# An attention-and-SwiGLU kernel on one Trainium2 core: the opening's order written out by hand, and one weight sum moved from tile zero to tile one

## The chip, the cores and the metric

One Trainium2 chip, one of its cores. The metric is the device time of one execution in microseconds. The kernel before takes 905.18 us, the median of three runs (903.3, 905.18 and 905.21).

The core has five engines with instruction streams of their own: TensorE (PE: matmuls and transposes), VectorE (DVE), ScalarE (ACT), GpSimd (POOL) and SyncE (SP), which here only issues DMA transfers. They wait for each other through semaphores.

## The reference

Chunked softmax attention, its heads joined to rows of 512 features, an RMS norm, and a SwiGLU layer:

```python
B, H, S, D = 8, 8, 576, 64; chunk = 64
# attention: each chunk of 64 tokens of a head looks at itself alone
scores = scale * np.matmul(q_c, k_c.transpose(0, 1, 2, 4, 3))   # 64 x 64 each
scores = scores - np.max(scores, axis=-1, keepdims=True)
attn = np.exp(scores)
attn = attn / (np.sum(attn, axis=-1, keepdims=True) + 1e-09)
out = np.matmul(attn, v_c)
x = out.reshape(B, H, S, D).transpose(0, 2, 1, 3).reshape(4608, 512)
# SwiGLU
rms = np.sqrt(np.mean(x * x, axis=-1, keepdims=True) + 1e-06)
xn = x / rms * rms_g
g = xn @ w_gate                       # 512 -> 1536
silu = g * (1.0 / (1.0 + np.exp(-g)))
val = xn @ w_val                      # 512 -> 1536
return silu * val @ w_out             # 1536 -> 512
```

All data are float32.

## The kernel before

**Tiles.** The 4608 tokens are cut into nine tiles of 512. Attention works in *units* of 256 tokens, two *subtiles* of 128 each: tile zero has units 0 and 1 (subtiles 0 to 3), tile one units 2 and 3, tile two units 4 and 5, and so on. The 1536 hidden features are twelve blocks f of 128.

**Precision.** Tokens and weights are split into a high and a low part (`xh`, `xl`; `parts` of a weight holds both), and a product takes three matmuls: high x high, high x low, low x high. One block `up(f)` is 24 matmuls, 12 for the gate (`ps_g`) and 12 for the value (`ps_v`). Then ScalarE takes the Silu of `ps_g` into `sg`, VectorE multiplies it with `ps_v`, ScalarE casts the high part `gh`, VectorE subtracts for the low part `gl`, and TensorE does `down(f)`, 12 matmuls into `acc`.

**Weights.** The weights arrive in 18 *pairs* in the order up f, up f+1, out f/2: one load of 1 MB each into a `raw` buffer (`conv_load`, issued AHEAD = 4 pairs ahead on SP's queue). Their conversion into parts takes these steps: ScalarE makes the absolute value (L189) and scales the low words (L190) in `conv_start`; VectorE clamps (L198), shifts (L199), joins the words (L200, L203) and ScalarE casts the high part (L214) in `conv_join`; VectorE subtracts for the low part (L220, the *remainder*) in `conv_end`. `conv_step` does the load for pair n+4, the start of pair n+1, the join of n and the end of n−1. Block up(f) needs the remainder of its pair. Buffers: 3 for `w`, 18 for `parts`, so that all converted weights stay on the chip.

**The opening.** q and k of unit 0 come in four pieces of 256 KB, q on SP's queue and k on ScalarE's (L254, L255). Subtiles 0 to 3 go through scores, softmax (a maximum and a subtraction on VectorE, one Exp on ScalarE, a sum on VectorE), transposes of the result, values, a scale by the sum (`norm`, L482), a sum of squares on ScalarE (L470), the mean on VectorE (L471), a power on GpSimd (L473), a scale on ScalarE (L488), transposes of the tokens (`x_transpose_unit`, L554) and their split (`x_split`: xh on ScalarE L523, xl on VectorE L524). The scores of subtiles 2 and 3 share one pair of PSUM banks (`s2`), two transposes of a unit share one buffer `eT`. No order is written down here: a list scheduler chooses each engine's order from the program below and from its own costs. `conv_step(EARLY)` with EARLY = 3 stands behind it.

```python
    s0, s1, s2 = (two_banks(p, "ps_s") for p in (ps_a, ps_h, ps_acc))
    scores(0, s0)
    scores(1, s1)
    softmax(0)
    softmax(1)
    ...
    x_transpose_unit(1)
    conv_start(0)
    conv_step(EARLY)
```

**Tile zero** is a plain loop over f: `gated(f)` (up, gate), pieces of the attention of unit 2 and unit 3, `save_out` and `save_up` (stores of converted weights for later tiles), the sums of output weights, `down(f-1)`. Within the loop the same list scheduler sets the order. Unit 2's four stages (scores with `softmax_rows`, transposes, values with `norm_unit`, scale) stand at f = 0, 2, 3, 4, unit 3's at 5, 7, 8, 9. `softmax_rows` has 32 Exp of 128x64 elements on ScalarE (L309), each with its sum; ScalarE loads another function table when it goes from Silu to Exp and back. `out_sides(i)` combines output weights of pair i for a later product: a sum (L659), four totals (L667), a cast (L671) and a remainder (L672). EARLY_SUMS = 2 of them stand in tile zero, at f = 9 and 10.

**Tiles one and two** run under `tc.manual_schedule`: within it each engine's order is that of the program text. They consist of 48 steps (`half`, called after each half block), and tables say at which step a piece of other work stands: UNIT_AT (eleven pieces for each of the units 4 to 9), SIDE_AT (sums of weights on GpSimd, `sides`), SUM_AT (the rest of `out_sides`). Behind them come three pairs of tiles whose matmuls are seven products in place of eight.

## Time and profile before

| | us | share of the span |
|---|---|---|
| median of three runs | 905.18 | |
| profiled execution | 903.54 | |
| its span | 901.8 | |
| PE busy | 875.2 | 97% |
| DVE busy | 672.1 | 75% |
| ACT busy | 438.1 | 49% |
| POOL busy | 171.6 | 19% |

The span reaches from the first to the last instruction that the profile shows in one profiled execution; that execution's own time is 1.7 us longer. Busy times are sums over the whole span, over stages with different limits, so the same engine can be idle in one stage and full in another. In the rows of the profile, a line begins with the start in microseconds (or with a stretch a:b), then the duration, engine, source line, operation and, in the form out<-in, the tiles; in square brackets stands how long the engine was idle just before, and what ended that. Rows of a stretch have the busy time of PE, PEld (weight loads), DVE, ACT and POOL, then the granted clock of TensorE, the busy share of the DMA engines and GB/s. Rows of groups end in the count.

### The profile page before, as it was taken

How to read it: one execution, taken by the hardware profiler on the slowest of the kernel's cores; microseconds unless marked ns; L12 is line 12 of the kernel's file. 1: busy time of each engine (PE TensorE's matmuls, PEld its weight loads, DVE VectorE, ACT ScalarE, POOL GpSimd, SP SyncE). 2: the span in 40 equal slices, each digit the busy share in tenths (PEclk: the TensorE clock that was granted, in tenths of full speed). 3: DMA queues.
4: the chain of work that ended last, by engine and by line, in shares of the span. 5: the costliest groups of instructions: out<-in, count | busy, mean ns of one | idle time of the engine just before them, and what ended most of it. 6: DMA issues, size and time to landing. Idle time of an engine off the chain costs nothing.

```text
span 901.8 us, 17138 instructions
## 1 busy us (share of the span) xinstructions
PE 875.2 (97%) x6792; PEld 715.4 (79%) x6792; DVE 672.1 (75%) x1083; ACT 438.1 (49%) x733; POOL 171.6 (19%) x213
## 2 busy tenths in 40 slices
PE   5799999999999999999999999999999999999998
PEld 4588878877888888888877888888878888888886
DVE  6999996788686887876577988756679974345885
ACT  5997944446353663433355644334536532112452
POOL 0100005395670000112221001122210002111000
PEclk9999999999999999999999999999999999999999
DMA  9698966879879967489877884898689677445623
GB/s 358 267 376 311 312 242 218 268 240 289 252 232 312 293 240 266 162 308 350 259 271 233 302 300 164 303 291 316 238 255 330 256 297 266 152 156 191 217 72 116
DMA packets 96512, 231.82 MB, mean 257 GB/s; under 512 B 7344, under 2 KB 63664, under 8 KB 81072
## 3 DMA queue, kind: packets, MB, share of 16 engines
q1 hardware_dynamic: 95376, 230.19, 73.9%
q8 instruction: 54, 0.88, 0.4%
q10 hardware_dynamic: 1056, 0.52, 0.2%
q14 instruction: 26, 0.21, 0.1%
HBM read 171.97 MB, written 58.72 MB: 256 GB/s over the span
## 4 chain that ended last, share of the span: by engine, by line
PE 74%; DVE 8%; issue 6%; ACT 6%; DMA 4%; POOL 1%; SPq 1%; ACTq 0%; DVEq 0%; POOLq 0%
PE ps_a L794 10%; PE ps_c L794 10%; PE ps_b L794 10%; PE ps_a L975 7%; PE ps_b L975 7%; PE ps_c L975 6%; PE ps_d L794 5%; PE ps_g L606 5%; PE ps_v L606 4%; PE ps_d L975 4%; PE ps_s L269 1%; PE ps_o L392 1%; DMA wr<-wsd 1%; PE acc L629 1%; DVE ab L723 1%
## 5 line engine op out<-in xcount | busy, mean ns | idle before, releaser
L894 ACT CAST gh<-g 128x512 fp32r<-128x512 f32 x140 | 81.7, 620 | 75.5 <-PE ps_b L975 21.3
L895 DVE TENSOR_TENSOR gl<-g,gh 128x512 fp32r<-128x512 f32 x140 | 95.3, 688 | 30.3 <-ACT gh L894 29.3
L794 PE MATMUL ps_c<-xp,wr 128*128 128x512 f32 x432 | 104.7, 391 | 0.0
L794 PE MATMUL ps_b<-xp,wr 128*128 128x512 f32 x432 | 104.4, 391 | 0.0
L794 PE MATMUL ps_a<-xp,wr 128*128 128x512 f32 x432 | 103.7, 390 | 0.4 <-DMA wr<-wsd 0.4
L794 PEld LDWEIGHTS ps_a<-xp,wr 128*128 128x128 f32 x432 | 80.9, 188 | 17.6 <-issue 0.8
L794 PEld LDWEIGHTS ps_c<-xp,wr 128*128 128x128 f32 x432 | 80.7, 188 | 17.1
L794 PEld LDWEIGHTS ps_b<-xp,wr 128*128 128x128 f32 x432 | 80.6, 188 | 16.9
L859 POOL TENSOR_TENSOR g<-c,c 128x512 f32<-128x512 f32 x18 | 23.2, 1291 | 359.1 <-DVE c L855 269.0
L606 PE MATMUL ps_g<-xh,parts 128*128 128x512 f32 x192 | 65.8, 396 | 1.1 <-ACT sg L619 1.1
L606 PE MATMUL ps_v<-xh,parts 128*128 128x512 f32 x192 | 66.2, 398 | 0.0
L975 PE MATMUL ps_a<-gh,wo 128*128 128x512 f32 x176 | 55.9, 389 | 0.0
L794 PE MATMUL ps_d<-xp,wr 128*128 128x512 f32 x216 | 51.9, 389 | 0.0
L975 PE MATMUL ps_c<-gh,wo 128*128 128x512 f32 x160 | 51.1, 392 | 0.2 <-ACT gh L894 0.2
L975 PE MATMUL ps_b<-gh,wo 128*128 128x512 f32 x160 | 50.5, 389 | 0.0
L794 PEld LDWEIGHTS ps_d<-xp,wr 128*128 128x128 f32 x216 | 40.5, 188 | 8.4
L937 DVE TENSOR_TENSOR g<-g 128x512 f32<-128x512 f32 x68 | 46.6, 686 | 0.0
L835 ACT ACTIVATE c<-c 128x512 f32<-128x512 f32 x18 | 11.4, 635 | 68.1 <-DVE c L855 68.0
L606 PEld LDWEIGHTS ps_v<-xh,parts 128*128 128x128 f32 x192 | 36.3, 189 | 10.1 <-issue 2.1
L606 PEld LDWEIGHTS ps_g<-xh,parts 128*128 128x128 f32 x192 | 36.5, 190 | 9.6 <-ACT sg L619 1.6
L844 DVE TENSOR_TENSOR u<-ps_b,p 128x512 f32<-128x512 f32 x36 | 24.0, 685 | 25.2 <-PE ps_b L794 24.0
L695 POOL TENSOR_TENSOR ab<-parts 128x256 f32<-128x256 f32 x48 | 37.3, 810 | 23.5 <-DVE xl L524 23.5
(176 smaller groups left out, 1872.3 us busy)
## 6 DMA issues: line engine op xcount, KB each, us to landing
wr<-wsd SPq DMA_DIRECT2D x63, 1024.0 KB, 8.5
qk<-qk_dram SPq DMA_DIRECT2D x17, 1024.0 KB, 6.9
wo<-wol SPq DMA_DIRECT2D x16, 1024.0 KB, 8.0
raw<-w_up_dram SPq DMA_DIRECT2D x12, 1024.0 KB, 13.0
wo<-wod SPq DMA_DIRECT2D x12, 1024.0 KB, 9.4
vt<-v_dram SPq DMA_DIRECT2D x18, 512.0 KB, 5.8
wsd<-parts SPq DMA_DIRECT2D x18, 512.0 KB, 8.3
wo<-wol SPq DMA_DIRECT2D x16, 512.0 KB, 7.6
```

Source lines behind the costliest of these rows:

```text
L269: nc.tensor.matmul(st["s"][j][c * CH : (c + 1) * CH, pr], st["q"][rows, pr, tok : tok + CH], st["k"][rows, pr, tok : tok + CH], start=True ...
L392: nc.tensor.matmul(st["o"][(2 * c + t) * Q : (2 * c + t + 1) * Q, h * D : (h + 1) * D], eT[rows, c, t, h], vt[rows, c, h], start=True, sto ...
L606: nc.tensor.matmul(ps[k], a, b[dt], start=(dt == 0 and i == 0), stop=(dt == NDT - 1 and i == 2), skip_group_check=True,)
L695: return nc.gpsimd.tensor_tensor(out, one, two, op=op)
L794: nc.tensor.matmul(ps, w[:, a, m, cols], xp[:, b, kt], start=start and kt == 0 and i == 0, stop=stop and kt == 1 and i == 2, skip_group_ch ...
L835: nc.scalar.activation(t, t if src is None else src, AF.Silu)
L844: nc.vector.tensor_tensor(kp["u2"], b["b"], kp["p1"], op=add)
L859: nc.gpsimd.tensor_tensor(g[1][1], kp["c22"], kept[0]["c22"], op=mult)
L894: nc.scalar.copy(gh, src)
L895: nc.vector.tensor_tensor(gl, src, gh.bitcast(F32), op=ALU.subtract)
L937: nc.vector.tensor_tensor(out, one, two, op=ALU.subtract)
L975: nc.tensor.matmul(ps[m][INTO[p]], w[:, m, a], parts[c], start=p in FROM and i == 0 and j == 0, stop=p in LAST and i == NPR - 1 and j == 2 ...
```

## The change

1. The opening is wrapped in a manual schedule of all five engines, and its text is written in a new order. Softmax is cut into `softmax_less`, `softmax_exp`, `softmax_sum` and `softmax_turned` (the reciprocal, once for both subtiles of a unit); `norm` into `norm`, `norm_square` and `norm_scale`; the conversion into `conv_abs`, `conv_low`, `conv_clamp`, `conv_words`, `conv_high`. The mean of squares is taken on GpSimd in front of the power.
2. q and k are laid out so that each subtile is one load of 512 KB (`load_sub`), four in all, all on SP's queue. The scores have four pairs of banks, and the transposes of the opening (`later=True`) go to buffers of `gh` and `gl`.
3. Only pair 0 is converted in the opening, and pair 1 is started. For pairs 2 to 7, ScalarE's first steps are ordered behind the last split of tokens (`tokens_first`).
4. `up_first` takes the place of `up` for f = 0: high x high of gate and value first, then low weights, then low tokens.
5. In tile zero, the stages of unit 2 stand at f = 1, 3, 4, 5 and of unit 3 at 6, 8, 9, 10 (UNITS_AT).
6. EARLY_SUMS goes from 2 to 1: `out_sides(0)` stands at f = 10, and `out_sides(1)` at step 2 of tile one.
7. Two rows of UNIT_AT (units 6 and 7) are changed, from their third number on by five to seven steps.

```diff
+UNITS_AT = {1: (2, 0), 3: (2, 1), 4: (2, 2), 5: (2, 3), 6: (3, 0), 8: (3, 1), 9: (3, 2), 10: (3, 3)}
 UNIT_AT = (
...
-    (5, 10, 16, 12, 14, 16, 25, 27, 27, 28, 31),
-    (11, 15, 27, 17, 19, 27, 32, 34, 34, 35, 38),
+    (5, 10, 13, 12, 14, 15, 18, 20, 20, 21, 25),
+    (11, 15, 20, 17, 19, 21, 26, 28, 28, 29, 32),
...
-SUM_AT = 0, 0, 7, 12, 26, 32
+SUM_AT = 0, 2, 7, 12, 26, 32
-EARLY_SUMS = 2
+EARLY_SUMS = 1
...
+    def tokens_first(ins, n):
+        if 1 < n <= LATER:
+            info = mybir.DependencyInfo(mybir.DependencyClass.NoSync, mybir.DependencyReason.DATA)
+            tc.add_manual_dep(ins.ins, first_last[0].ins.name, info, reason="tokens are split first")
...
+    def load_sub(i, t):
+        t = t.rearrange("p (w a t) -> p w a t", w=2, t=P)
+        nc.sync.dma_start(t, qk[i // 2][:, i % 2])
+        state[i] = {"q": t[:, 0], "k": t[:, 1]}
...
+    def up_first():
+        pg, pv = bank(ps_h, "ps_g"), bank(ps_h, "ps_v")
+        for i in range(3):
+            for ps, wh, wl in ((pg, wgh, wgl), (pv, wvh, wvl)):
+                a, b = ((wh, xh), (wl, xh), (wh, xl))[i]
+                for dt in range(NDT):
+                    nc.tensor.matmul(ps, a[0][:, dt * P : (dt + 1) * P], b[dt], ...)
+        return pg, pv
...
+    first_ordered = tc.manual_schedule(engines={*engines, mybir.EngineType.Pool})
+    first_ordered.__enter__()
+    for i in range(2):
+        load_sub(i, x[:, 2 * i : 2 * i + 2].rearrange("p s c -> p (s c)"))
+    t = io.tile([P, 2, 2, NPAIR, P], F32, tag="qk", bufs=1, name="qk")
+    for s in range(2):
+        load_sub(2 + s, t[:, s].rearrange("p w a t -> p (w a t)"))
+    load_values(0)
     conv_load(0)
+    nc.sync.dma_start(g_col, rms_g)
     load_values(1)
+    for n in range(1, AHEAD + 1):
         conv_load(n)
+    s0, s1, s2, s3 = (two_banks(p, "ps_s") for p in (ps_a, ps_h, ps_acc, ps_acc))
     scores(0, s0)
     scores(1, s1)
+    for i in range(2):
+        softmax_less(i)
+        softmax_exp(i)
+    copied = att_transpose(0, later=True)
+    scores(2, s2)
+    softmax_sum(0)
+    copied()
+    copied = att_transpose(1, later=True)
+    scores(3, s3)
+    softmax_sum(1)
+    softmax_turned(0)
+    copied()
+    softmax_less(2)
+    softmax_exp(2)
+    conv_abs(0)
...
+    att_values(3, o)
+    norm_scale(0)
+    norm(2)
+    norm_square(2)
+    norm_scale(1)
+    for half in range(2):
+        x_transpose_half(0, half, ps_a)
+    norm(3)
+    norm_square(3)
+    conv_words(0)
+    x_split_half(0, 0)
+    norm_scale(2)
+    x_split_half(0, 1)
+    conv_high(0)
+    norm_scale(3)
+    for half in range(2):
+        x_transpose_half(1, half, ps_acc)
+    conv_end(0)
+    for half in range(2):
+        x_split_half(1, half)
+    conv_start(1)
+    first_ordered.__exit__(None, None, None)
+    conv_step(EARLY - 1)
...
     for f in range(NF):
         g = gated(f, CONVS[f % 2], conv_step)
-        if f in (0, 5):
-            u = 2 + (f == 5)
+        u, stage = UNITS_AT.get(f, (None, None))
+        if stage == 0:
```

In the rows below the operation of an engine stands with its line, its output and inputs, the shape, and how often it stands in a row; line numbers of the two kernels differ. TensorE, from the last transposes of the opening into up(0), before; `xh_119` to `xh_122` are the high parts of the four blocks of 128 features, `xl_123` to `xl_126` the low ones:

```order
L554 MATMUL ps_x<-ident,x 128x128 x8
L565 MATMUL ps_g<-xh_119,parts 128x512
L565 MATMUL ps_v<-xh_119,parts 128x512
L565 MATMUL ps_g<-xl_123,parts 128x512
L565 MATMUL ps_g<-xh_119,parts 128x512
L565 MATMUL ps_v<-xl_123,parts 128x512
L565 MATMUL ps_v<-xh_119,parts 128x512
L565 MATMUL ps_g<-xh_120,parts 128x512
L565 MATMUL ps_v<-xh_120,parts 128x512
L565 MATMUL ps_g<-xl_124,parts 128x512
```

and after:

```order
L597 MATMUL ps_x<-ident,x 128x128 x16
L627 MATMUL ps_g<-xh_119,parts 128x512
L627 MATMUL ps_v<-xh_119,parts 128x512
L627 MATMUL ps_g<-xh_120,parts 128x512
L627 MATMUL ps_v<-xh_120,parts 128x512
L627 MATMUL ps_g<-xh_121,parts 128x512
L627 MATMUL ps_v<-xh_121,parts 128x512
L296 MATMUL ps_s_564<-qk 64x64 x2
L296 MATMUL ps_s_565<-qk 64x64
L627 MATMUL ps_g<-xh_122,parts 128x512
L627 MATMUL ps_v<-xh_122,parts 128x512
L627 MATMUL ps_g<-xh_119,parts 128x512
```

Before, up(0) takes the three products of one feature block after another; now it takes the high products of all four blocks first and the low parts of the tokens last, and the scores of unit 2 begin within it. The last eight transposes of the tokens stood alone ahead of it, and now all sixteen stand there together.

ScalarE, tile zero, around the 32 Exp of unit 2 (`e`, by rows of scores in two banks), before:

```order
L583 ACTIVATE sg<-ps_g 128x512
L309 ACT_TABLE_LOAD
L309 ACTIVATE e,rs_u<-ps_s_509,mx_u 128x64 x4
L309 ACTIVATE e,rs_u<-ps_s_510,mx_u 128x64 x3
L588 CAST gh<-sg 128x512
L309 ACTIVATE e,rs_u<-ps_s_510,mx_u 128x64
L309 ACTIVATE e,rs_u<-ps_s_509,mx_u 128x64 x4
L309 ACTIVATE e,rs_u<-ps_s_510,mx_u 128x64 x4
L214 CAST parts<-w 128x1024
L189 ACTIVATE w<-raw 128x1024
L583 ACT_TABLE_LOAD
L583 ACTIVATE sg<-ps_g 128x512
```

and after:

```order
L344 ACT_TABLE_LOAD
L344 ACTIVATE e,rs_u<-ps_s_564,mx_u 128x64
L649 ACT_TABLE_LOAD
L649 ACTIVATE sg<-ps_g 128x512
L344 ACT_TABLE_LOAD
L344 ACTIVATE e,rs_u<-ps_s_564,mx_u 128x64
L654 CAST gh<-sg 128x512
L344 ACTIVATE e,rs_u<-ps_s_564,mx_u 128x64 x2
L344 ACTIVATE e,rs_u<-ps_s_565,mx_u 128x64 x4
L344 ACTIVATE e,rs_u<-ps_s_564,mx_u 128x64 x4
L344 ACTIVATE e,rs_u<-ps_s_565,mx_u 128x64 x4
L237 CAST parts<-w 128x1024
```

A Silu (`sg`) now stands within the block of Exp, behind its first one, with a table load on each side of it; before, the Silu stood ahead of the block. The Exp block also stands later in the row of casts of `parts` and weight steps (`w`).

SyncE, its queue of loads and stores from weight pair 3 on (counted from 0) (`raw` is a weight load, `qk` and `vt` q, k and v of a unit, `wsd` and `wod` stores of converted weights), before:

```order
L181 DMA raw<-w_up_dram 128x1024 x2
L181 DMA raw<-w_out_dram 128x1024
L239 DMA qk<-qk_dram 128x2048
L181 DMA raw<-w_up_dram 128x1024 x2
L245 DMA vt<-v_dram 128x1024
L688 DMA wod<-parts 128x2048
L181 DMA raw<-w_out_dram 128x1024
L239 DMA qk<-qk_dram 128x2048
L245 DMA vt<-v_dram 128x1024
L685 DMA wsd<-parts 128x4x256
```

and after:

```order
L183 DMA raw<-w_up_dram 128x1024 x2
L269 DMA qk<-qk_dram 128x2048
L183 DMA raw<-w_out_dram 128x1024
L275 DMA vt<-v_dram 128x1024 x2
L751 DMA wsd<-parts 128x4x256
L183 DMA raw<-w_up_dram 128x1024
L269 DMA qk<-qk_dram 128x2048
L183 DMA raw<-w_up_dram 128x1024
L754 DMA wod<-parts 128x2048
L183 DMA raw<-w_out_dram 128x1024
L183 DMA raw<-w_up_dram 128x1024
```

In both the first row is pairs 3 and 4. Unit 2's q and k now stand ahead of pair 5 instead of behind it. Pair 6 now stands behind the values of unit 3 and the first store `wsd`, which stood behind pair 8 before, and pair 7 behind unit 3's q and k, which also stood behind pair 8; the store `wod` is still ahead of pair 8.

More of the change, by code (lines that the diff above doesn't have):

```diff
@@ new lines, in conv_high @@
+    def conv_high(n):
+        w = conv[n][2]
+        parts = wts.tile([P, 2, 2, DM], F32R, tag="wts", name="parts")
+        (conv_parts if pairs[n][0] == "up" else out_parts).append(parts)
+        conv[n] = w, parts
+        kind, f = pairs[n]
+        if kind == "up":
+            homes = (wgh, wgl, f), (wvh, wvl, f)
+        else:
+            homes = (woh, wol, f), (woh, wol, f + 1)
+        for i, (hi, lo, at) in enumerate(homes):
+            hi[at], lo[at] = parts[:, 0, i], parts[:, 1, i]
+        nc.scalar.copy(parts[:, 0].rearrange("p i c -> p (i c)"), w)
@@ L289, in softmax_sum, with softmax_turned @@
         st = state[i]
[L290 to L291 removed]
+        if i % 2 == 0:
+            state["rs", i // 2] = small.tile([P, 2, NPAIR, 2, 1], F32, name="rs")
+        st["rs"] = state["rs", i // 2][:, i % 2]
+        nc.vector.tensor_reduce(st["rs"], st["e"], axis=AX.X, op=ALU.add)
+    def softmax_turned(u):
+        rs = state.pop(("rs", u))
         nc.vector.tensor_scalar_add(rs, rs, 1e-9)
@@ L572, in up @@
         return ps
-    def gated(f, at, then):
-        pg = up(wgh, wgl, f, "ps_g")
-        pv = up(wvh, wvl, f, "ps_v")
+    def up_first():
[4 more added lines that the diff above has]
+                for dt in range(NDT):
+                    nc.tensor.matmul(
+                        ps,
+                        a[0][:, dt * P : (dt + 1) * P],
+                        b[dt],
+                        start=(dt == 0 and i == 0),
+                        stop=(dt == NDT - 1 and i == 2),
+                        skip_group_check=True,
+                    )
+        return pg, pv
+    def gated(f, at, then):
+        if f == 0:
+            pg, pv = up_first()
+        else:
+            pg = up(wgh, wgl, f, "ps_g")
+            pv = up(wvh, wvl, f, "ps_v")
         if 0 in at:
```

194 lines of the change are left out of this document (94 added, 100 removed).

## The prediction

> **What bounds the kernel now.** I read the page first, then the busy time by stage, cut at the places where TensorE's work changes: its first up matmul (34.4 us), the first of tile one (144.8) and the first of tile two (224.5).
>
> ```profile
> span 901.8 us, 17138 instructions
> ...
> PE 875.2 (97%) x6792; PEld 715.4 (79%) x6792; DVE 672.1 (75%) x1083; ACT 438.1 (49%) x733; POOL 171.6 (19%) x213
> ```
> ```profile
> 0.00:34.40 34.40, 18.35 (x288) 13.86 (x288) 25.52 (x58) 23.05 (x37) 4.44 (x11) 1.00 0.96 377
> 34.40:144.80 110.40, 108.82 (x721) 89.05 (x722) 104.95 (x142) 87.70 (x163) 2.75 (x2) 1.00 0.80 286
> 144.80:224.50 79.70, 76.39 (x802) 61.39 (x800) 61.77 (x113) 39.38 (x61) 54.01 (x72) 0.98 0.77 251
> ```
>
> TensorE (third column) is busy 97% of the span, so only its waits and its start are to be had: 34.40 - 18.35 = 16.0 us in the opening, 1.6 in tile zero, 3.3 in tile one. But in tile zero VectorE (fifth column) is busy 104.95 of 110.40: it converts the weights there, and a second engine is as full as the bound. The waits of TensorE, from its own list:
>
> ```profile
> 4.88 1.13 PE L269 MATMUL ps_s<-x 64*64 64x64 f32 x32 [4.88 <-DMA x<-qk_dram]
> ...
> 33.10 1.11 PE L554 MATMUL ps_x<-ident,x 128*128 128x128 f32 x4 [3.53 <-ACT x L488]
> 34.42 0.80 PE L565 MATMUL ps_g<-xh,parts 128*128 128x512 f32 x1 [0.20 <-ACT xh L523]
> ```
> ```profile
> 123.83 0.50 PE L565 MATMUL ps_g<-xh,parts 128*128 128x512 f32 x1 [1.57 <-ACT sg L583]
> ...
> 132.12 0.39 PE L565 MATMUL ps_g<-xh,parts 128*128 128x512 f32 x1
> ```
> ```profile
> 144.79 0.39 PE L606 MATMUL ps_g<-xh,parts 128*128 128x512 f32 x1
> ```
> ```profile
> 190.37 0.39 PE L606 MATMUL ps_v<-xl,parts 128*128 128x512 f32 x1 [1.92 <-issue]
> ```
>
> Up(0) starts at 34.42, up(11) at 132.12, tile one at 144.79. In between one wait of 1.57 us counts.
>
> **The opening, step by step.** Durations are start to start in a row of back-to-back instructions.
>
> ```profile
> 7.79 0.76 DVE L282 TENSOR_REDUCE mx<-ps_s 128x4 f32<-128x256 f32 x2 [0.34 <-PE ps_s L269]
> ...
> 9.13 1.47 DVE L291 TENSOR_REDUCE rs<-e 128x8 f32<-128x512 f32 x2
> ...
> 13.54 0.75 DVE L482 TENSOR_TENSOR x<-ps_o,rs 128x256 f32<-128x256 f32 x2
> ```
> ```profile
> 30.16 0.61 ACT L470 ACTIVATE e<-x 128x512 f32<-128x512 f32 x1
> ...
> 32.33 0.72 ACT L488 ACTIVATE x<-x,ri 128x512 f32<-128x512 f32 x1 [0.42 <-POOL ri L473]
> 32.96 1.03 ACT L214 CAST parts<-w 128x1024 fp32r<-128x1024 f32 x1
> 33.89 0.84 ACT L523 ACTIVATE xh<-ps_x,g_col 128x256 fp32r<-128x256 f32 x2
> 34.63 2.21 ACT L190 ACTIVATE raw<-raw 128x1024 int32<-128x1024 uint32 x2
> ```
> ```profile
> 31.13 1.16 POOL L473 TENSOR_TENSOR ri<-ss,mhalf 128x1 f32<-128x1 f32 x1 [3.69 <-DVE ss L471]
> ```
>
> The first 512 KB of q and k come as one transfer instead of two on two queues, and I leave the first scores at 4.88: that cost is 0, bounded by half of the 4.88 either way. Softmax of a subtile takes VectorE about 1.4 us (7.79 to 9.13 and the overlap), so the first two are done at 9.2, as now. In the new order two sums and a reciprocal follow (1.8), then the softmax of subtiles 2 and 3, to 12.4 and 14.2. TensorE does values 0 from 12.7, values 1 to 16.1 (1.13 each, transposes of 1.1 between), values 3 to 19.4; each norm (0.67) follows its values, the last at 20.1. ScalarE then sets the pace: square 3 ends at 21.4, GpSimd's add and power take about 1, and between them ScalarE has four xh copies (0.37), a scale (0.63) and cast 0 (0.93). Scale 3 ends near 25.5, the transposes behind it give the first xh at about 26.4. There TensorE starts up(0): 8.0 us before its 34.42. Four banks for the scores, and four for the transposes, take away the waits on the earlier softmax; they cost nothing. The sum of squares moves its add to GpSimd, about 0.2 us inside that 1.
>
> **What those 8 us are worth.** The last split of tokens on VectorE is over at 28.3, and pair 1's first step follows its Abs at 28.9. From there VectorE has no room:
>
> ```profile
> 40.28 1.22 DVE L220 TENSOR_TENSOR parts<-w,parts 128x1024 fp32r<-128x1024 f32 x1
> 41.41 1.22 DVE L203 CUSTOM_DVE_ANT_0 w<-raw,w 128x2048 uint16<-128x2048 uint16 x1
> 42.55 0.69 DVE L587 TENSOR_TENSOR sg<-ps_v,sg 128x512 f32<-128x512 f32 x1
> 43.15 0.69 DVE L198 TENSOR_SCALAR w<-w 128x1024 f32<-128x1024 f32 x1
> 43.75 0.69 DVE L303 TENSOR_REDUCE mx_u<-ps_s 128x8 f32<-128x512 f32 x1
> ```
> ```profile
> 62.87 1.23 DVE L220 TENSOR_TENSOR parts<-w,parts 128x1024 fp32r<-128x1024 f32 x1
> ...
> 72.70 1.42 DVE L498 TENSOR_TENSOR x<-ps_o,rs_u 128x256 f32<-128x256 f32 x4
> ...
> 128.14 1.22 DVE L220 TENSOR_TENSOR parts<-w,parts 128x1024 fp32r<-128x1024 f32 x1
> ...
> 131.08 1.22 DVE L659 TENSOR_TENSOR w<-parts 128x1024 f32<-128x1024 f32 x1
> ...
> 132.81 1.09 DVE L667 TENSOR_TENSOR w<-w 128x256 f32<-128x256 f32 x3
> ...
> 135.22 1.22 DVE L672 TENSOR_TENSOR parts<-w,parts 128x1024 fp32r<-128x1024 f32 x1
> ```
>
> A pair costs three steps of 1.14 and two of 0.60, 4.62 us. Up to the remainder (L220) of pair 16, the last that up(11) needs, the new order has 16 pairs after pair 0 (73.9), 1.2 of pair 17, 20 gate instructions of 0.60 (12.0), four maxima (2.4), five norms of 0.33 (1.7) and about 0.8 of small ones: 92.0 us. To them come waits. The largest is at unit 2: its 16 Exp now stand later, split by a Silu, with two table loads more, and cast 6 stands behind the last of them.
>
> ```profile
> 39.55 1.28 ACT L583 ACT_TABLE_LOAD   x1
> ```
> ```profile
> 48.12 2.19 ACT e L309 x14
> ```
>
> The second row is seven Exp with their sums, 0.31 each. Following both engines, the last Exp ends at 66.5, cast 6 at 67.5, so pair 6's remainder comes at 68.6 where now it is done at 64.0, though TensorE started 8 us sooner. All waits together I put at 3.4 us: pair 16 at 28.9 + 92.0 + 3.4 = 124.3, now 129.3 (128.14 + 1.14). So VectorE lets tile zero gain 5.0, not 8.0.
>
> TensorE from pair 6 on: the rest of up(4) to 73.1, values 1.1, up(5) 5.45 and down(4) 2.72 to 82.4; up(6) waits for pair 9 until 83.5. Three ups, four downs and 3.0 us of scores, transposes and values follow, with 0.7 us of waits for pairs 12 and 13, and up(11) starts near 127.6: 4.5 us before its 132.12. That the scale of unit 3 now stands before the last Silu instead of before f=9's is in it: the 1.57 us wait goes, since Silu(11) has two matmul blocks in hand. At the end of the tile the remaining sum (1.14 + 4 x 0.36 + 1.14 = 3.7 us) and the later scale press on the last gate; I give back 0.7. Tile one starts 3.8 us earlier.
>
> The other sum of 3.7 us goes into tile one's steps 2 to 5, where VectorE is idle 79.70 - 61.77 = 17.9 us over the tile and waits for the scores of unit 5 right behind it: cost 0.3, bounds 0 and 3.7. Units 6 and 7 move six to seven steps earlier. That is 1.3 + 1.25 us of VectorE, two squares, two scales on ScalarE and 1.5 us of TensorE taken from tile two: hidden while the split for tile two stays behind TensorE, which then also arrives 1.5 us later. Bounds 0 and 3; I take 0. Work behind tile two stays in its order.
>
> The sum: 3.8 - 0.3 = 3.5 us. The profiled execution took 903.54 for its 901.8 span; 903.54 - 3.5 = 900.0. The median of the runs, 905.18, lies 1.6 above it: 901.7, and I say 901.5.
>
> **The rivals.** *A stall that comes or goes.* At 190.37 TensorE waited 1.92 us for nothing that the profile shows ("issue"), and its granted clock (third from the right) fell afterwards:
>
> ```profile
> 120.00:130.00 10.00, 8.43 (x37) 6.65 (x37) 10.00 (x14) 4.94 (x7) 1.68 (x1) 1.00 0.59 214
> ```
> ```profile
> 191.00:192.00 1.00, 1.00 (x4) 0.76 (x4) 0.93 (x4) 1.00 (x4) 0.92 (x3) 0.60 1.10 249
> 192.00:193.00 1.00, 1.00 (x3) 0.78 (x3) 1.00 (x3) 0.74 (x2) 0.83 (x3) 0.50 0.79 209
> ```
>
> Four slices (191 to 195, two of them shown) at 0.5 to 0.7 lose about 1.7 us more, 3.6 together. It stands behind a burst of small matmuls while transfers are at full share; the new program meets that place at another moment. Without it: 901.5 - 3.6 = 897.9. Chance 0.23; against it speaks that the burst itself is unchanged.
>
> *Waits that halve the clock.* In the new tile zero TensorE waits for VectorE near up(1), up(3) and up(4), 1 to 2 us each, by my chain; the wait of 1.57 us at 123.83 left the clock at 1.00, that of 1.92 did not. Two such drops at 1.7 us, partly inside the next wait, give 2: 903.5. Chance 0.12. [...]
>
> *Weights that come too late: slower.* Loads of raw pairs 6 to 9 now stand on the queue behind a store that waits for pair 0, the load of unit 3 and a store that waits for pair 2.
>
> ```profile
> raw<-w_up_dram SPq DMA_DIRECT2D x8, 1024.0 KB, 14.5
> ```
> ```profile
> raw<-w_out_dram SPq DMA_DIRECT2D x1, 1024.0 KB, 8.2
> ```
> ```profile
> 41.91 0.43 SPq L181 DMA_DIRECT2D raw<-w_out_dram  x1
> ```
>
> Pair 8's load would be issued at about 42 again, but its first step is now at 51 on ScalarE, in front of a gate. At 8.2 us of landing it is in time by 1; at the 14.5 of crowded loads it is 5.5 late, and cast 5, the Exp block and pair 6 shift with it, one for one: 907. It decides from a lateness of 3.7 us. Few bytes are in flight at 42, so chance 0.10.
>
> *TensorE keeps all 8 us* (pairs early enough after all): 905.18 - 8 = 897. The full VectorE column speaks against it; 0.05.
>
> *The new opening is no earlier*: an in-order wait on the first loads or on GpSimd holds it past 30, and VectorE's 92 us start as late as now. Then only the removed sum and the 1.57 us wait are left, less the Exp block: 904.5. Chance 0.08.
>
> **How the numbers follow.** The likeliest case, 901.5 (its own range 899.5 to 903.3), has 0.42. A difference under 0.2%, 1.8 us, is about what a measurement of this kernel can't tell from none. Faster: 0.42 + 0.23 + 0.05 and a little of the clock case, 0.72. Within: the clock case and the late opening, 0.16. Slower: late weights and a rest, 0.12. The range reaches from 896, the two early cases, to 905.5, and leaves out the late weights.
>
> **What would show it.** Right: up(0) near 26.4; VectorE at 95% or more from 29 to 125; pair 6's remainder near 68.6; up(11) near 127.6; tile one near 141. Wrong: up(0) past 30; pair 8's first step waiting for a transfer; a clock under 1.00 in tile zero; in tile one a longer wait for Silu than the present ones, or a wait for xl before tile two.

## The result and the profile after

The changed kernel takes 913.35 us (median of four runs, 912.56 to 914.83), the kernel before, in the same comparison, 904.73. The ratio is 1.0100, interval 1.0082 to 1.0118: it is slower by 8.6 us. The profiled execution took 913.26 for a span of 911.5, which is 9.7 more than the span before. That is 1.1 more than the medians differ: the profiled execution of before (903.54) lies 1.2 under the median of its runs, that of after at its median, so differences taken from the two traces can be about 1 us too large in sum. Page of after:

```profile
span 911.5 us, 17152 instructions
...
PE 881.0 (97%) x6792; PEld 714.5 (78%) x6792; DVE 677.2 (74%) x1075; ACT 442.6 (49%) x737; POOL 176.1 (19%) x217
```

TensorE does the same 6792 matmuls, but is busy 5.8 us longer: part of the loss is not a wait at all. The same events as in the prediction (timeline of TensorE, after: first up, up(11), first matmul of tile one):

```profile
29.49 0.80 PE L627 MATMUL ps_g<-xh,parts 128*128 128x512 f32 x1
```
```profile
133.57 0.40 PE L612 MATMUL ps_g<-xh,parts 128*128 128x512 f32 x1
```
```profile
147.02 0.40 PE L672 MATMUL ps_g<-xh,parts 128*128 128x512 f32 x1
```

Against before, the first up is 4.9 us earlier, up(11) 1.5 later and tile one 2.2 later. The lag is 5.2 where tile two ends. Of the 4.5 that come behind it, 4.1 are worked out below, from the three pairs' down stages; the last 0.4 are not assigned. Busy time by stage, after (columns: sum, then PE, PEld, DVE, ACT, POOL, then granted clock, DMA share, GB/s):

```profile
0.00:29.50 29.50, 15.79 (x289) 12.60 (x289) 19.10 (x42) 16.19 (x29) 6.06 (x15) 0.80 0.94 368
29.50:147.00 117.50, 113.45 (x722) 88.83 (x721) 108.83 (x144) 99.42 (x173) 3.29 (x2) 0.98 0.77 279
147.00:226.00 79.00, 73.61 (x910) 59.46 (x909) 63.86 (x115) 37.86 (x60) 57.02 (x75) 0.98 0.77 256
```

In tile zero TensorE was idle 1.6 us before, and is now idle 4.0; its busy time there grew too, from 108.8 to 113.5. Over tiles one and two it is busy 151.2 us, as before (151.1), and idle 6.4 in place of 3.6: what these two tiles lose are waits.

The granted clock under 1.00 in the first two rows is one stretch, from the last values of the opening into up(0) (TensorE alone):

```profile
17.40:34.55 17.15, 11.35 (x96) 0.50 1.02 414
```

At half clock the first matmuls of up(0) start 0.43 us or more apart instead of 0.23. Before, the first ones had that distance too, from 34.42 to 37.24, although the row of before gives 1.00 there: its trace has no record of the clock ahead of 37.6. Without the scores in between, up(0) takes 8.1 us now and 7.3 before. That difference stands ahead of a wait of 0.9 us for pair 1 (at 41.18), which would be the longer without it.

### The profile page after: what moved, and what is told of

Read it like the earlier page. It is cut to its first block, busy times and chain, and to the rows that moved or that the text cites. A ratio compares the mean times of both kernels' runs of the same rounds, so it can differ in the third digit from the quotient of the medians.

```text
span 911.5 us, 17152 instructions
## 1 busy us (share of the span) xinstructions
PE 881.0 (97%) x6792; PEld 714.5 (78%) x6792; DVE 677.2 (74%) x1075; ACT 442.6 (49%) x737; POOL 176.1 (19%) x217
## 4 chain that ended last, share of the span: by engine, by line
PE 73%; DVE 11%; ACT 6%; POOL 3%; DMA 3%; issue 3%; SPq 1%; DVEq 0%; ACTq 0%; POOLq 0%
PE ps_a L860 10%; PE ps_c L860 10%; PE ps_b L860 10%; PE ps_a L1041 7%; PE ps_b L1041 7%; PE ps_c L1041 7%; PE ps_d L860 5%; PE ps_g L672 4%; PE ps_v L672 4%; PE ps_d L1041 4%; POOL ab L761 2%; PE ps_s L296 2%; PE ps_o L438 1%; DVE w L220 1%; DVE parts L249 1%
## 5 line engine op out<-in xcount | busy, mean ns | idle before, releaser
L761 POOL TENSOR_TENSOR ab<-parts 128x256 f32<-128x256 f32 x48 | 37.8, 824 | 34.8 <-DVE e L408 13.8
L901 ACT ACTIVATE c<-c 128x512 f32<-128x512 f32 x18 | 11.4, 633 | 67.6 <-DVE c L921 67.5
L761 POOL TENSOR_TENSOR ab<-ab 128x256 f32<-128x256 f32 x48 | 41.9, 879 | 2.8
```

The source lines that it names most:

```text
L761: return nc.gpsimd.tensor_tensor(out, one, two, op=op)
L901: nc.scalar.activation(t, t if src is None else src, AF.Silu)
```

## The experiments

Four causes were possible: the opening and tile zero; the sum in tile one; the two rows of UNIT_AT; and the three pairs, whose text and order are unchanged. "Edit" is against after unless another base is named. Ratios are against the kernel before, run on the same chip.

| run | us | ratio [interval] |
|---|---|---|
| pad128 | 909.31 | 1.0057 [1.0045, 1.0069] |
| before_pad384 | 908.43 | 1.0045 [1.0033, 1.0057] |
| pad384 | 908.98 | one run |
| sum_back | 911.72 | 1.0083 [1.0067, 1.0098] |
| unit_back | 911.99 | 1.0089 [1.0073, 1.0104] |
| sum_unit_back | 909.39 | 1.0059 [1.0045, 1.0074] |
| before_sum1 | 905.77 | 1.0018 [1.0009, 1.0027] |
| three_back | 904.97 | 1.0005 [0.9996, 1.0014] |
| two_banks | 913.53 | 1.0102 [1.0089, 1.0115] |
| units_old | 917.06 | 1.0142 [1.0128, 1.0155] |
| opening_fixed | 905.30 | 1.0013 [1.0005, 1.0022] |
| late_pe | 906.09 | 1.0018 [1.0009, 1.0027] |
| fill | 905.15 | 1.0004 [0.9992, 1.0016] |
| urgent_only | 917.44 | 1.0160 [1.0137, 1.0182] |
| exp_early | 912.71 | 1.0104 [1.0090, 1.0118] |
| exp_early_f0 | 914.19 | 1.0120 [1.0104, 1.0135] |
| exp_early_fill | 903.10 | 0.9999 [0.9990, 1.0009] |
| fill_u2 | 901.99 | 0.9977 [0.9966, 0.9987] |

### The three pairs: where `gh` and `gl` lie

The opening's new small tiles make the pool `small` 128 bytes smaller per partition. The pools allocated behind it (`gp` with `gh` and `gl`, `tmp` with `sg`, and the buffers of `w` and `side`) move down by that: `gh` and `gl` start 64 bytes past a multiple of 512 where they started 192 past one; the weights stay at 192. These places follow from the sizes of the pools; the trace shows no addresses. Stretches of 40 us inside the down stages of the three pairs, TensorE alone (sum, busy and matmuls, clock, DMA share, GB/s); first before, then after:

```profile
500.00:540.00 40.00, 40.00 (x178) 1.00 0.85 311
690.00:730.00 40.00, 40.00 (x179) 1.00 0.71 261
855.00:895.00 40.00, 40.00 (x179) 1.00 0.26 93
```
```profile
500.00:540.00 40.00, 40.00 (x174) 1.00 0.91 315
690.00:730.00 40.00, 40.00 (x174) 1.00 0.80 286
855.00:895.00 40.00, 40.00 (x174) 1.00 0.20 69
```

There are no waits and the granted clock is 1.00 in both, yet four to five matmuls fewer fit into 40 us. From start to start a matmul takes 232.2 ns after and 226.7 before; three stages of 252 matmuls make 3 x 252 x 5.5 ns = 4.1 us. The DMA share does not matter here: the third stretch has 0.20 and as few matmuls.

pad128 gives the 128 bytes back:

```diff
+    pad = ctx.enter_context(tc.tile_pool(name="pad", bufs=1))
+    pad.tile([P, 32], F32, name="pad")
     gp = ctx.enter_context(tc.tile_pool(name="gp", bufs=2))
```

> The changed kernel with one unused tile of 128 bytes per partition ahead of the pool of gh and gl, so that gh, gl, sg, w and side stand at the byte addresses (modulo 512) that they have in the kernel before; no instruction is added. Theory (addresses): in the trace of the changed kernel the matmuls of the last three down stages follow each other every 232.2 ns where the kernel before has 226.7 ns; if it is the addresses of their operands, these stages go back to 226.7 ns, and 3 x 252 x 5.5 ns = 4.1 us are won: 909.2 us. Rival (another cause, such as the order of the queues or the throttle): 232 ns stay, 913.3 us.

before_pad384 is the counter-test: the same pad with 96 elements in the kernel *before*, which puts `gh` and `gl` at 64 past 512.

> The kernel before with an unused tile of 384 bytes per partition in the same place, which gives gh, gl, sg, w and side the addresses modulo 512 that they have in the changed kernel. Theory (addresses): its last three down stages slow from 226.7 to about 232 ns a matmul, 908.8 us. Rival (another cause): 226.7 ns, 904.7 us.

Both came out: pad128 is 4.0 us under after, before_pad384 is 4.0 over before (908.43 against 904.48 in its comparison). First pad128, then before_pad384:

```profile
500.00:540.00 40.00, 40.00 (x178) 1.00 0.92 318
690.00:730.00 40.00, 40.00 (x178) 1.00 0.80 287
```
```profile
500.00:540.00 40.00, 40.00 (x174) 1.00 0.90 312
690.00:730.00 40.00, 40.00 (x174) 1.00 0.75 272
```

pad384 (96 elements in after) puts `gh` and `gl` at 448 past 512, to tell 512 from 256:

> The changed kernel with 384 bytes of padding ahead of gh and gl: they then stand at 448 modulo 512 (192 modulo 256), the weights as ever at 192 modulo 512. 64 modulo 512 was slow (232 ns a matmul), 192 fast (226.7 ns). If the fast place is 192 modulo 256, the last three down stages run at 226.7 ns; if it has to be 192 modulo 512, they run at about 232 ns.

It took 908.98 in its single run, where pad128 takes 909.31. So by the times 192 and 448 are the quick places and 64 (913.35) the slow one. 192 and 448 are the place of the weights modulo 256, but the weights were never moved, so whether the distance to them counts or the place by itself was not tested. Nor was it separated which two accesses meet, since `sg`, `w` and `side` move with `gh`.

### The sum in tile one, and the rows of UNIT_AT

The chain in tile one of after, by the timelines of SyncE, GpSimd, VectorE and TensorE:

```profile
164.44 1.78 SPq L742 DMA_DIRECT2D wol<-parts  x2
```
```profile
DMA to landing us min/median/max: 7.3/7.4/7.5
```
```profile
173.31 7.93 POOL L761 TENSOR_TENSOR ab<-parts 128x256 f32<-128x256 f32 x8 [13.77 <-DVE e L408]
```
```profile
178.93 3.06 DVE L733 TENSOR_TENSOR w<-w 128x256 f32<-128x256 f32 x4
181.90 1.28 DVE L452 TENSOR_TENSOR xu<-ps_o,rs 128x512 f32<-128x512 f32 x2
```
```profile
183.40 0.33 PE L296 MATMUL ps_s<-qk 64*64 64x64 f32 x4 [1.98 <-ACT ps_o L508]
184.05 1.44 PE L296 MATMUL ps_s<-qk 64*64 64x64 f32 x60 [0.33 <-ACT ps_o L508]
```
```profile
183.00:184.70 1.70, 0.98 (x47) 1.00 0.15 39
184.70:188.20 3.50, 3.50 (x39) 0.51 0.59 200
```

The moved sum writes its result into the `parts` buffer of an output pair, and the two stores of it (issues at 164.4 and 165.7, 7.5 us to land: 173.2) hold that buffer. GpSimd's second batch of side sums (`ab<-parts`) needs it and starts at 173.31. The row names a VectorE instruction that ends at the same moment; the chain above and before_sum1 below say that it is the landing. Before, the batch ran from 157.26, and VectorE's totals and the norm of unit 5 had no neighbour:

```profile
157.26 5.59 POOL L695 TENSOR_TENSOR ab<-parts 128x256 f32<-128x256 f32 x8
```
```profile
173.18 1.81 DVE L667 TENSOR_TENSOR w<-w 128x256 f32<-128x256 f32 x4
174.90 1.28 DVE L406 TENSOR_TENSOR xu<-ps_o,rs 128x512 f32<-128x512 f32 x2
```

Beside GpSimd's adds the four totals take 3.06 us instead of 1.81. The norm comes at 181.90; with the 2.2 us by which tile one starts later it would have been 177.1. TensorE then waits 1.98 + 0.33 us for scores, and runs 3.5 us at half clock (0.51), which by that clock costs another 1.7. Before, the stall of 1.92 us ahead of 190.37 is followed by as long a stretch at half clock (0.50 from 191.2 to 194.6), so the difference between the two kernels lies in the waits.

sum_back moves only the sum back into tile zero, unit_back only the two rows, sum_unit_back both:

```diff
-EARLY_SUMS = 1
+EARLY_SUMS = 2
-SUM_AT = 0, 2, 7, 12, 26, 32
+SUM_AT = 0, 0, 7, 12, 26, 32
```
```diff
-    (5, 10, 13, 12, 14, 15, 18, 20, 20, 21, 25),
-    (11, 15, 20, 17, 19, 21, 26, 28, 28, 29, 32),
+    (5, 10, 16, 12, 14, 16, 25, 27, 27, 28, 31),
+    (11, 15, 27, 17, 19, 27, 32, 34, 34, 35, 38),
```

> The changed kernel with both sums of output weights in tile zero again (EARLY_SUMS = 2, SUM_AT[1] = 0). Theory (the sum holds a buffer): in the changed kernel GpSimd's second batch of side sums starts at 173.3 instead of 157.3 us, at the moment in which the store of the moved sum lands (issued at 165.7, 7.5 us), collides with the third sum on VectorE (four totals in 3.06 us instead of 1.81), and TensorE waits 2.3 us for the scores of unit 6 and drops to half clock for 3.4 us. With the sum back the batch starts about 14 us after the start of tile one again, and that wait and its drop go; the sum costs 1 to 3 us at the end of tile zero. Net 911 to 913 us, tiles one and two 2.5 to 4 us shorter. Rival (the steps of units 6 and 7 crowd tile one): the wait of 2 us for the scores stays, and the time rises by the cost of the sum, 914 to 916 us.

> The changed kernel with the two rows of UNIT_AT for units 6 and 7 as before; the moved sum stays in tile one. Theory (the moved sum holds a buffer of GpSimd, and the earlier steps of units 6 and 7 are a second, smaller cause): the 2 us wait for the scores of unit 6 near 183 and its half clock stay, the waits for unit 7's transfers near 214 (1.0 us) go: 912 to 913 us. Rival (the earlier steps of units 6 and 7 alone lengthen tile one): the wait near 183 goes, 910 us.

> The changed kernel with both sums in tile zero and the two rows of UNIT_AT as before, so that tiles one and two have the text of the kernel before. With the sum alone back, the wait for the scores went and another came: 2.4 and 1.3 us for the transfers of units 6 and 7, with 6.8 us of half clock. Theory (both parts together cost tiles one and two their 3 us): their length is that of the kernel before within 0.5 us, 910 us. Rival (the length of these tiles hangs on when they start against the stores of tile zero, not on their text): 911.5 us or more.

TensorE's waits in tile one, in after, then sum_back, then unit_back (total, times, longest):

```profile
PE ps_s L296 <- ACT ps_o L508: 2.3, 2, 2.0
PE ps_v L672 <- issue: 2.1, 1, 2.1
PE ps_o L438 <- DMA eT<-away_e: 1.0, 1, 1.0
```
```profile
PE ps_o L438 <- DMA eT<-away_e: 3.7, 2, 2.4
```
```profile
PE ps_s L296 <- ACT ps_o L508: 2.6, 2, 2.3
```

With the sum away the wait for scores is gone, but with the new rows the values of the next units then wait 3.7 us for the transfer that brings their transposed softmax: one wait takes the place of the other, and each edit alone is worth only 1.4 to 1.6 us. With both back neither wait is left (a wait for Silu of 2.9 us stands there in the profiled execution, 1.1 before), and 4.0 us are won (909.39). By the traces half of that lies in tiles one and two: from the start of the one to the end of the other sum_unit_back takes 155.7 us, after 157.6 and before 154.7, so 1.0 is left where its expectation allowed 0.5. Of the rest, 0.6 lies in the opening, whose text is the same, and 0.7 in tile zero.

before_sum1 is the kernel before with the sum moved and nothing else:

> The kernel before with only the sum moved: EARLY_SUMS = 1, SUM_AT[1] = 2. Theory (the moved sum's store holds the buffer that GpSimd's second batch of side sums needs): that batch starts about 14 us later than 157.3, and tile one grows by 2 to 4 us, with a wait for the scores of unit 6 and a half clock; tile zero ends 0 to 1 us earlier; 906 to 908 us. Rival (the late batch harmed only together with the new steps of units 6 and 7): 904 to 905 us.

It takes 905.77, 1.2 us more, a little under what the theory expected. There TensorE waits up to 1.5 us for scores, and the waits of GpSimd name the store:

```profile
POOL ab L695 <- DMA wol<-parts: 12.4, 1, 12.4
```

### All three undone, the opening left as it is

three_back is after with pad128, the sum and the rows together. If the opening gained what was predicted, it would be under before by 3.8; if these three are the whole loss, level with it.

> The changed kernel with the addresses, both sums and the rows of units 6 and 7 as before, and its opening and tile zero untouched. If the causes add up: 913.35 - 4.0 (addresses) - 3.7 (sum and rows) = 905.6 us, about 1 us over the kernel before, which is then what the opening and tile zero cost. If opening_fixed owed its 905.3 to the splits over two banks, 907 us.

904.97 against 904.62: level. The three account for the whole loss, within the noise, and the opening and tile zero, from which the gain was to come, are worth nothing: 0.4 us slower, with an interval of -0.4 to +1.3.

### Why an earlier first up is worth nothing

Busy time in tile zero, before and then after (columns as above):

```profile
20.00:34.00 14.00, 7.38 (x84) 4.97 (x82) 12.83 (x28) 13.53 (x22) 2.62 (x2) 1.00 1.01 417
34.00:60.00 26.00, 25.80 (x170) 20.64 (x169) 25.07 (x35) 25.78 (x58) 0.00 (x0) 1.00 0.71 266
60.00:72.00 12.00, 12.00 (x113) 9.80 (x112) 11.85 (x14) 10.51 (x13) 0.00 (x0) 1.00 1.03 363
```
```profile
20.00:34.00 14.00, 8.55 (x31) 5.56 (x32) 9.52 (x17) 9.81 (x19) 3.46 (x4) 0.50 1.02 413
34.00:60.00 26.00, 23.86 (x154) 18.54 (x152) 25.68 (x31) 22.90 (x25) 0.00 (x0) 0.99 0.79 285
60.00:72.00 12.00, 11.16 (x51) 8.44 (x49) 10.38 (x15) 11.91 (x40) 0.00 (x0) 1.00 0.85 285
```

Before, VectorE and ScalarE are both full while TensorE is still in the opening: between 20 and 34 they are idle 1.2 and 0.5 us, because pair 1 is already being converted there. After, they are idle 4.5 and 4.2. ScalarE then is idle 3.1 of the next 26 us, where it was 0.2, and its Exp block comes after 60. TensorE's start moved, the conversion did not. (The 40 instructions of ScalarE in the last row include unit 2's block. It has 16 Exp, each with a read of its sum; the 32 of the description above counts both. The block ran from 48.1 to 53.4 before, ahead of the cast of pair 4, and from 62.7 to 71.3 after, ahead of the cast of pair 6.)

The opening itself, ScalarE and VectorE, after:

```profile
24.15 0.47 ACT L568 ACTIVATE xh<-ps_x,g_col 128x256 fp32r<-128x256 f32 x1 [0.98 <-DVE xl L569]
```
```profile
24.66 0.48 DVE L569 SCALAR_TENSOR_TENSOR xl<-ps_x,g_col,xh 128x256 fp32r<-128x256 f32 x1 [0.54 <-ACT xh L568]
...
32.94 0.69 DVE L212 TENSOR_SCALAR w<-w 128x1024 f32<-128x1024 f32 x1 [0.54 <-ACT w L190]
```

Two feature blocks share a bank of transposes, and ScalarE's `xh` of the second waits for VectorE's `xl` of the first; the two engines go in turns, 0.5 to 1.0 us each time. two_banks takes the first blocks of both banks, then the second ones:

```diff
-    x_split_half(0, 0)
+    x_split_one(0, 0, 0)
+    x_split_one(0, 1, 0)
     norm_scale(2)
-    x_split_half(0, 1)
+    x_split_one(0, 0, 1)
+    x_split_one(0, 1, 1)
...
-    for half in range(2):
-        x_split_half(1, half)
+    for i in range(2):
+        for half in range(2):
+            x_split_one(1, half, i)
```

> The changed kernel with the eight splits of the opening's tokens taken alternately from the two PSUM banks (blocks 0, 2, 1, 3) in place of one bank after the other (0, 1, 2, 3). Theory (an in-order bank): in the changed kernel xh of the second block of a bank waits for xl of the first, on the other engine, 0.54 to 0.98 us each, four times; the list scheduler of the kernel before had alternated the banks. The first up matmul comes 0.5 to 1.5 us earlier than 29.49, the first step of pair 1 on VectorE 1.5 to 2.5 us earlier than 32.94, and since VectorE paces tile zero the time falls by 1.5 to 2.5 us, to about 911.3. Rival (the opening's lateness does not reach the end, tile zero is held by something else): within 0.5 us of 913.3.

The turns go and the first up starts at 27.80, 1.7 earlier, but the time stays, as the rival said (913.53): by the trace pair 1 is done 2.4 us earlier, pair 13 still 1.1, and pair 16 no longer (129.9, against 129.7 in after). units_old puts the stages of units 2 and 3 back at the old f (UNITS_AT with 0, 2, 3, 4 and 5, 7, 8, 9):

> The changed kernel with the stages of units 2 and 3 at f = 0, 2, 3, 4 and 5, 7, 8, 9 again. In the changed kernel tile zero loses 7.0 us from its first up matmul to its last, although VectorE is busy over 96% of it. Theory (the Exp blocks stand where pairs 6 and 13 need ScalarE, and VectorE waits 1.5 us for each): with the old stages tile one starts 1 to 2 us earlier, 911.3 to 912.3 us. Rival (VectorE's 96.8 us from pair 1 to pair 16 alone decide): tile one starts within 0.5 us of 147.0, 913 us.

A miss with the opposite sign: 917.06, 3.7 slower than after. With the new opening the later stages help.

opening_fixed is three_back with the order of two_banks. From here on it is the base:

> The changed kernel with the addresses of the kernel before (128 bytes of padding), both sums in tile zero, the old rows of units 6 and 7, and the splits of the opening alternating between the two banks; what is left of the change is the opening's order, its loads, up_first and the later stages of units 2 and 3. If the three causes add up (4.1 us addresses, 3.0 us tiles one and two, nothing for the splits), 906.2 us, 1.7 us over the kernel before, all of it in tile zero. If the earlier start of the splits reaches the end of tile zero now, 904 to 905 us. If the causes overlap (less half clock to be won twice), 907.5 us.

905.30: 0.5 to 2.0 us over before by the interval, between the sum of the three causes (906.2) and a gain that reaches the end (904 to 905). late_pe delays only TensorE in it, by 24 transposes more whose result nobody reads; the first up starts at 32.75 instead of 27.94:

> The kernel opening_fixed with 24 more transposes (their output is not used) on TensorE behind the token transposes, so that up(0) starts 2 to 4 us later while VectorE and ScalarE have the same opening. Theory (VectorE paces tile zero, TensorE's early start is worth nothing): tile one starts within 1 us of the time that it has in opening_fixed, 904.5 to 906.3 us. Rival (an earlier up(0) is worth its time, less what VectorE takes): 907 us or more.

906.09, 0.8 over opening_fixed, and tile one starts at 145.12 against 145.63: 4.8 us of TensorE's start are worth at most 0.8. fill instead converts pair 1 within the gaps of the opening (`conv_abs(1)` behind `norm_scale(0)`, `conv_clamp(1)` behind `conv_words(0)`, `conv_low(1)` ahead of `conv_high(0)`, `conv_words(1)` behind `norm_scale(3)`, `conv_high(1)` behind the last split):

> The kernel opening_fixed with pair 1 converted within the opening: its Abs, low words, clamp, shift and words stand in gaps of ScalarE and VectorE between 19 and 30 us. Theory (VectorE sets the pace from its first instruction on, and an hour of its idle time in the opening costs an hour at pair 16): up to pair 16 VectorE was busy 115.5 us of 130.1 in opening_fixed, with 3.1 us idle from 20 to 34; with 2 us of that filled, pair 16 ends near 128 and tile one starts 1.5 to 2 us earlier, though up(0) starts 0.5 to 2 us later: 903 to 904 us. Rival (the start of up(0) counts): 906 us or more. Second rival (the Exp blocks and the order within tile zero hold pair 16 wherever VectorE stands at 34): 905.3 us.

Pair 1 is done at 34.8 instead of 38.8, and still pair 16 ends at 130.3, against 130.1: 905.15, the second rival. So the start of VectorE's work does not set the pace either. The remainder of pair 16 in after and in fill:

```profile
128.51 1.22 DVE L249 TENSOR_TENSOR parts<-w,parts 128x1024 fp32r<-128x1024 f32 x1
```
```profile
129.06 1.22 DVE L251 TENSOR_TENSOR parts<-w,parts 128x1024 fp32r<-128x1024 f32 x1
```

Pair 1's first step on VectorE stands at 24.2 in fill, 30.7 in two_banks, 30.8 in opening_fixed, 32.9 in after and 33.2 in three_back, and in all five pair 16 is done between 129.7 and 130.3. Of fill's lead of 4.0 us, 1.0 is left at pair 2 and 0.5 at pair 5; what takes it that early was not followed. The rest goes at pair 6 (fill, then fill_u2, below):

```profile
60.00:72.00 12.00, 9.97 (x45) 7.30 (x45) 9.21 (x13) 11.93 (x40) 0.00 (x0) 1.00 0.97 322
```
```profile
60.00:72.00 12.00, 11.58 (x92) 9.04 (x91) 11.89 (x15) 11.80 (x14) 0.00 (x0) 1.00 0.90 305
```

In fill, ScalarE is full between 60 and 72, mostly with unit 2's Exp block, and VectorE is idle 2.8 us; it waits for the Exp and for cast 6 behind them. Four runs move the Exp forward, by a higher priority for the softmax of units 2 and 3 (`with urgent(): softmax_rows(u, sc)`): urgent_only in after, exp_early in opening_fixed, exp_early_f0 with the old UNITS_AT as well, exp_early_fill in fill.

> The changed kernel with the softmax of units 2 and 3 in tile zero at high priority, and nothing else: its Exp instructions stand together again, after one table load, and unit 2's come after the second Silu instead of around 61 us. Theory (ScalarE's Exp block sets pair 6): in the changed kernel the block runs from 61.4 to 70.9 us with two table loads more than before, after ScalarE had been idle 3.0 us from 50 to 60, and pair 6 ends at 73.5 instead of 64.0; with an early block pair 6 ends 4 to 6 us earlier, tile one starts 2.5 to 5 us earlier, 908.5 to 911 us. Rival (VectorE's total of work holds pair 16): pair 16 stays at 129 to 130, 912.5 us or more.

> The kernel opening_fixed with the softmax of units 2 and 3 in tile zero at high priority. Theory (ScalarE's Exp block sets pair 6): pair 6 ends near 66 instead of 71.5, tile one starts 2.5 to 5 us earlier than its 145.6, 901 to 903 us, faster than the kernel before. Rival (VectorE's total): 905 us.

> The kernel exp_early with the stages of units 2 and 3 at f = 0, 2, 3, 4 and 5, 7, 8, 9, as before. Without the priority these places cost 3.7 us (units_old). Theory (what cost there was the order of ScalarE, not the place): within 1.5 us of exp_early. Rival (the earlier places cost by themselves): 3 us or more over it.

> The kernel fill (pair 1 converted within the opening) with the softmax at high priority. In fill alone pair 1 came 4.0 us earlier and pair 6 no earlier (71.7). Theory: with the Exp block out of the way the 1.45 us of idle time that fill takes from VectorE count now: 900 to 902 us, 1 to 1.5 us under exp_early. Rival (ScalarE is full from 30 to 50 anyway): the same as exp_early.

Without the filled opening, Exp first is a loss, against the expectations of both runs: 4.1 us in urgent_only (917.44 against 913.35), 7.4 in exp_early (912.71 against 905.30), and about 1 us more by the ratios, since the kernel before ran at 903.59 in their comparison. In urgent_only unit 2's Exp run from 43.4 to 48.2, ahead of the cast of pair 2, and TensorE waits for remainders of the weights; TensorE in tile zero of urgent_only:

```profile
PE ps_g L612 <- DVE parts L249: 5.7, 3, 4.3
```

The place of the stages hardly matters there: exp_early_f0, at the old f, is within 1.5 us of exp_early. In exp_early the largest wait is another, 7.1 us of the transposes of units 2 and 3 for their Exp, 4.8 of it unit 2's; why the scheduler put them so early there was not followed. With the filled opening it is 903.10, level with before (903.59 there) and 1 us over what was expected. fill_u2 raises only unit 2:

```diff
-            softmax_rows(u, sc)
+            if u == 2:
+                with urgent():
+                    softmax_rows(u, sc)
+            else:
+                softmax_rows(u, sc)
```

> The kernel exp_early_fill with high priority for unit 2's softmax alone. In exp_early_fill pair 6 came at 68.5 instead of 71.7, but VectorE was idle 4.5 us between 100 and 129, 2.6 more than in fill, around unit 3's Exp. Theory (both converting engines pace tile zero, each idle microsecond of VectorE counts at pair 16): with unit 3 as in fill pair 16 ends near 125 and tile one starts 1 to 2 us earlier than its 144.4: 901 to 902.5 us, faster than the kernel before. Rival (unit 3's block holds pair 13 at 115 wherever pair 6 comes): pair 16 at 127 or later, 903 us or more.

901.99 against 904.62, 0.9977 [0.9966, 0.9987]: faster than both kernels, by 2.6 us over before. Its first up starts at 30.40, later than in opening_fixed, and tile one at 143.38, 1.4 before the kernel before. The remainder of pair 6 in after, then in fill_u2:

```profile
72.39 1.23 DVE L249 TENSOR_TENSOR parts<-w,parts 128x1024 fp32r<-128x1024 f32 x1 [0.47 <-ACT parts L237]
```
```profile
67.72 1.22 DVE L251 TENSOR_TENSOR parts<-w,parts 128x1024 fp32r<-128x1024 f32 x1
```

Neither the filled gap (fill) nor the early Exp of both units (exp_early) gains anything alone; fill with unit 2's Exp early does, and then pair 6 is 4.7 us earlier and pair 16, done at 127.9, 1.8. That is the time that was expected, but pair 16 was expected near 125, and 127 or later belonged to the rival. Unit 2's priority without the filled opening was not run, so it is not shown that this gain needs both. Why the same priority for unit 3 takes part of it back stays open.

## Why the prediction was wrong, point by point

The forecast was a gain of 3.5 us; it became a loss of 8.6. In the spans, it missed three terms: 6.0 at the start of tile one (-3.8 forecast, +2.2 measured), 2.7 in tiles one and two (+0.3, +3.0), and 4.1 in the three pairs (0). The last two are shown by runs that take them out; of the first, the runs show that the forecast gain did not exist, and only in part why.

**"Work behind tile two stays in its order", cost 0: 4.1 us.** The order did stay. What moved was the place of the buffers in memory, which the order does not show and the prediction did not look at. It is in none of the rivals. The experiments show this term in both directions, out of after and into before.

**"The other sum ... cost 0.3, bounds 0 and 3.7", and the rows of UNIT_AT, "bounds 0 and 3; I take 0".** Together 4.0 us (909.39 against 913.35). The sum was priced by VectorE's time, and VectorE had room, as said. The price lay in its result: a store that holds a buffer, which GpSimd waits for 12 us (12.4 in before_sum1). "Who waits for the buffer that this step writes" was not asked. Both ends of the bounds were set from the engine alone, so the row that mattered (GpSimd's `ab`) was not among them. Of the new rows the price shows as the 3.7 us for transfers in sum_back; they were taken as hidden. The wait for xl ahead of tile two, which the forecast named as a sign of being wrong, came as well: 1.0 us, 0.3 before.

**"There TensorE starts up(0): 8.0 us before".** It starts 4.9 before. The term that was mis-sized is "four xh copies (0.37)": each second copy waits for the other engine's read of the bank, 0.98, 0.55, 0.55 and 0.58 us in the row of ScalarE. GpSimd's add and power, "about 1", took 1.03 + 1.63 for the third square, and 0.22 + 0.57 for the next, a moment later:

```profile
21.40 1.03 POOL L510 TENSOR_SCALAR ms<-ms 128x1 f32<-128x1 f32 x1 [1.68 <-ACT e L508]
```

TensorE's transposes wait 1.77 and 2.26 us for the scales behind them. But the error cost nothing: two_banks starts 1.7 us earlier for the same time, and late_pe 4.8 later for at most 0.8.

**"What those 8 us are worth": "pair 16 at 28.9 + 92.0 + 3.4 = 124.3".** The direction was right: VectorE, not TensorE, was named as what lets tile zero gain less. But pair 16 was done at 129.73 and tile one started at 147.02 instead of 141. In after the row of work has the forecast size, 95.4 us from pair 1's first step to pair 16 and 96.8 measured (32.94 to 129.73), and the start is wrong, 28.9 forecast and 32.94 measured, because the last splits go in turns too. That looks as if the late start explained the miss, and it does not. The step that failed is the sum itself, which passes an earlier start on to pair 16 one for one ("from there VectorE has no room"). Where the runs moved the start, the row grew or shrank by as much: 99 us in two_banks and opening_fixed, 106 in fill, with pair 16 always at 129.7 to 130.3. That the row fits in after is luck.

What holds pair 16 there is shown only in part. One piece is ScalarE's Exp block, ahead of cast 6. It was in the forecast, a cast 6 at 67.5, and ended at 72.35; by the forecast's own chain 4.0 of these 4.9 us are the late start. Against the kernel before, the remainder of pair 6 starts 9.5 us later, of which by pair 16 only 0.4 is left:

```profile
61.42 1.28 ACT L344 ACT_TABLE_LOAD   x1
...
63.14 1.28 ACT L649 ACT_TABLE_LOAD   x1
...
65.05 1.28 ACT L344 ACT_TABLE_LOAD   x1
...
71.23 1.12 ACT L237 CAST parts<-w 128x1024 fp32r<-128x1024 f32 x1
```

Two table loads more were foreseen; only one of them falls ahead of cast 6 (four from 20 us on, three before), 1.28 us. The forecast did not count ScalarE's own idle time from 20 to 60: 7.3 us against 0.7 (14.00 - 9.81 and 26.00 - 22.90, against 14.00 - 13.53 and 26.00 - 25.78). That and the load are 7.9 of the 9.5; the rest is other work of ScalarE that now stands ahead of cast 6, a Silu and two steps of later weights among it. This is an account of where ScalarE's time went, not a test. The prediction called VectorE the second bound and gave ScalarE free room, though its rows in the opening were as full; fill, which puts pair 1 earlier and leaves the Exp block where it is, gains nothing, and fill_u2, which moves the block as well, has pair 16 done 2.4 us earlier than fill. In the gap of the opening both engines had converted pair 1 before.

**The removed sum and the 1.57 us wait.** The wait for Silu did go. The sum that left tile zero gave nothing there: in sum_back, which has it again, tile zero is 0.6 us shorter than in after, not longer.

**The rivals.** Late weights did not occur: no conversion in tile zero waits for a `raw` load. The stall at 190 came again, shifted:

```profile
196.80 0.39 PE L672 MATMUL ps_v<-xh,parts 128*128 128x512 f32 x1 [2.06 <-issue]
```

This time the clock stayed at 1.00 behind it. A clock under 1.00 in tile zero, which the forecast named as a sign of being wrong, came at its start: half clock from 17.5 on, in the last part of a wait of 1.72 us that ends at 17.75, until 34.55; TensorE is busy 11.35 of the 17.15 us from 17.4 on. The rival looked for it behind waits within tile zero, and those (1.22 us the longest) did not lower the clock, which is 1.00 from 34.55 to 184.7. In tile one half clock followed on waits of 1.98 and 0.33 us, for 3.5 us. With two stalls of about 2 us, of which one (1.98 us) was followed by half clock and one (2.06 us) was not, the length of a wait alone does not decide it here.

## What to carry to other kernels

Where TensorE is busy nearly all the time but a conversion feeds it, as here, starting TensorE sooner can be worth nothing. An earlier start of the conversion need not help either, if something behind it holds its end: look at the fill of *all* the engines that convert, and where their long blocks (Exp with its table loads) fall, before pulling the start. When a step moves, follow the buffer it writes to its last reader, stores included, and ask which engine wants it next. And after any change of pools compare the addresses of the matmul operands: a loss that is spread evenly over stages whose order is unchanged, at full clock and without waits, was of that kind here, and one unused tile tests it.
